# Attention and two expert layers on one core: sums of `s` in two runs, weight sums on VectorE, output products placed later, nine early products

## The chip, the core and the metric
The kernel runs on one core of a Trainium2 chip. The core has five engines that run side by side, each in the order of its own instructions: TensorE (products, "PE" in the profile), VectorE (DVE), ScalarE (ACT), GpSimd (POOL) and SyncE (SP, which here only issues transfers). Semaphores order them. The metric is device time in microseconds of one launch, measured outside the profiler; lower is better.

## The reference
```python
def _attn_ref(q, k, v, s):                     # (4, 8, 576, 64), s: (4, 8, 576)
    scores = scale * np.matmul(q, k.transpose(0, 1, 3, 2))
    cum = np.cumsum(np.maximum(s, 0.0), axis=-1)
    bias = -(cum[:, :, :, None] - cum[:, :, None, :])
    scores = np.where(causal, -1000000000.0, scores + np.minimum(bias, 0.0))
    ...
    attn = attn / (np.sum(attn, axis=-1, keepdims=True) + 1e-09)
    return np.matmul(attn, v)

x = attn_out as 2304 tokens of 512
h = np.maximum(x @ w_in, 0.0);  x = h * h @ w_out                        # w_in 512 x 2048
h = np.maximum(np.maximum(x @ w1, x @ w2), x @ w3);  out = h @ w_out2    # w1 512 x 768
```
The matrices of the two expert layers arrive as 64-bit words, which the kernel turns into pairs of tiles (a high and a low part).

## The kernel before, in words
**Attention.** The 32 heads are taken as 16 pairs. Each pair has nine units of query rows; `u_s` computes the scores of a unit on TensorE: first the product of `xq` and `xk`, and on top of it a product of `cq` and `ck` (line 646), three rows of bf16 parts of the cumulated sum of `s` for each head and three rows of constants, which adds the bias. `u_max` (VectorE), `u_exp` (ScalarE), `u_t` (transposes on TensorE), `u_et` (ScalarE) and `w_pv` follow; the numbers of `ORDER` set how many units each is late.

`setup` makes the sums. VectorE scales `s`, scans its 576 columns (32 heads on 32 partitions), and splits the result into three bf16 parts. The first pair gets its rows of `ck` and `cq` straight from these (`cum(parts)`: three transfers on SP's queue, three on ScalarE's). All parts are also stored to `c_dram`, and every later pair reads its rows from there. After that `v()` loads the pair's values, and `loads(1)` the second pair's keys, queries, rows of `c_dram` and values, all on SP's queue and in that order.

**Weights.** A weight tile is a job of nine to eleven stages: load of 64-bit words (`st`), four VectorE steps (`exponent` to `rest`, lines 397 to 408), a sum of two tiles (`whole`, line 415), ScalarE's cast to the high part (line 429), and a subtraction that leaves the low part (line 433). The sum and the subtraction run on `adder[0]`: GpSimd in the attention stage, VectorE after (`adder[0] = nc.vector` at the head of `experts`). `Slots` decides when the stages are issued. Jobs that are begun in the attention stage keep what `w_job` read when they were begun.

**First expert layer.** For each block of tokens and each block `f` of 128 hidden units, TensorE does twelve products into a bank (`h_products`, line 812), ScalarE and VectorE turn the bank into `hh` (lines 971 to 974: relu, square, high part, low part), and TensorE does twelve products of `hh` with `w_out` (line 995), two blocks later (`LAG`).

**Second expert layer.** Three groups of 768 tokens. A group has nine items (three weight matrices in three column pairs); an item has seven product steps of six products of 384 columns (line 1132), with 1, 5 and 2 copied out of their bank by ScalarE (`s1`, `s5`, `s2`) and added by VectorE. After its nine items a group has six output tiles of 128 tokens: `split_out` makes high and low part (`hh`), 18 products (line 1104) follow, the result is copied to `ob` and stored on SP's queue. `OUT2_AT` says between which steps of the next group's items an output tile stands: {item: {step: tile}}. The last group's tiles come at the end. `split_out` of a tile is issued after the tile ahead of it.

## Time and profile before
| | |
|---|---|
| runs | 847.57, 847.71, 850.11 us (median 847.71) |
| profiled execution | 847.02 us, of which the span of the core is 845.2 us |
| TensorE busy | 826.4 us (98%), 5284 products |
| VectorE, ScalarE, GpSimd busy | 524.3, 407.5, 175.4 us |
| attention, first layer, second layer, by TensorE's lines | about 0 to 174, 174 to 566, 566 to 842 us |

Times in the rows are microseconds from the start of the span unless marked ns. A row of a timeline has the start, the length, the engine, the line of the program, the operation, what it writes and reads by the program's names, the tile's size, and a count; in brackets stands how long the engine had been idle and what ended that. Rows of the same kind that follow each other are merged. SPq rows are issues of transfers; their length is the issue alone (or from the first issue to the end of the last, where several are merged). TensorE's products overlap, and their ends are modelled.

### The profile page before, as it was taken

Reading aid. Unit: us, or ns where it says so; the run is one execution under the profiler, and the core shown is the slowest. Engines: PE = TensorE matmul, PEld = TensorE weight load, DVE = VectorE, ACT = ScalarE, POOL = GpSimd, SP = SyncE. Lnnn points to the kernel's source line nnn. Section 1 sums busy time; section 2 is a strip of 40 time slices with the busy share of each in tenths; the row PEclk is TensorE's granted clock in tenths of the full one; section 3 lists DMA queues with packets and bytes.
Section 4 is the critical chain, followed back from the end, with each engine's and each line's share of the span. In section 5 each row is a group of like instructions: output and inputs, shape, how many; then the busy total and the mean of one; then the engine's idle time right before and its main releaser. Section 6 shows DMA issues by size and latency. Waiting matters only on the chain.

```text
span 845.2 us, 14494 instructions
## 1 busy us (share of the span) xinstructions
PE 826.4 (98%) x5284; PEld 700.5 (83%) x5284; DVE 524.3 (62%) x1103; ACT 407.5 (48%) x833; POOL 175.4 (21%) x273
## 2 busy tenths in 40 slices
PE   5999999999999999999999999999999999999998
PEld 3555565577888899999998888889998899899996
DVE  6777787749766656765877786843563335633442
ACT  5888889845544445445544555432242222421221
POOL 3054444544231323222123232100000000000000
PEclk9999999999999999999999999999999999999999
DMA  5565657453544454896758596639921573026602
GB/s 162 178 192 170 218 188 217 123 154 126 179 153 148 150 194 150 310 362 218 243 201 309 181 314 228 248 105 406 407 91 44 197 262 121 13 75 217 231 1 75
DMA packets 72631, 159.77 MB, mean 189 GB/s; under 512 B 12784, under 2 KB 32816, under 8 KB 72560
## 3 DMA queue, kind: packets, MB, share of 16 engines
q1 hardware_dynamic: 55764, 102.73, 36.1%
q0 software_dynamic: 16784, 56.11, 18.8%
q8 instruction: 41, 0.67, 0.3%
q14 instruction: 30, 0.25, 0.1%
q10 hardware_dynamic: 12, 0.01, 0.0%
HBM read 113.53 MB, written 45.27 MB: 188 GB/s over the span
## 4 chain that ended last, share of the span: by engine, by line
PE 91%; DVE 3%; ACT 2%; DMA 2%; POOL 1%; issue 0%; SPq 0%; DVEq 0%; ACTq 0%; POOLq 0%
PE banks L995 22%; PE banks L1132 13%; PE first L812 11%; PE banks L812 11%; PE banks L1104 9%; PE first L1132 8%; PE pairs L768 5%; PE pairs L723 3%; PE pairs L644 2%; PE pair L644 2%; PE pair L651 1%; ACT e L681 1%; DMA st<-in_w_in_dram 1%; PE pairs L651 1%; DVE hh L807 1%; PE pairs L646 1%
## 5 line engine op out<-in xcount | busy, mean ns | idle before, releaser
L995 PE MATMUL banks<-hh,sl 128*128 128x512 f32 (+1 forms) x960 | 210.1, 367 | 1.8 <-DVE hh L974 1.8
L995 PEld LDWEIGHTS banks<-hh,sl 128*128 128x128 f32 x960 | 175.1, 188 | 24.8 <-DVE hh L974 2.2
L1132 PE MATMUL banks<-xs,sl 128*128 128x384 f32 x702 | 131.2, 335 | 0.0
L1132 PEld LDWEIGHTS banks<-xs,sl 128*128 128x128 f32 x702 | 122.8, 188 | 0.9 <-DMA sl<-keep_p 0.2
L974 DVE TENSOR_TENSOR hh<-r,hh 128x512 fp32r<-128x512 f32 (+1 forms) x80 | 52.0, 651 | 98.8 <-ACT hh L973 98.6
L812 PE MATMUL first<-xs,sl 128*128 128x512 f32 (+1 forms) x432 | 93.6, 365 | 0.0
L812 PE MATMUL banks<-xs,sl 128*128 128x512 f32 (+1 forms) x432 | 93.6, 365 | 0.0
L681 ACT ACTIVATE e<-e,nm 128x128 f32<-128x128 f32 (+2 forms) x144 | 83.5, 585 | 10.0 <-DVE nm L667 9.9
L812 PEld LDWEIGHTS first<-xs,sl 128*128 128x128 f32 x432 | 78.6, 188 | 9.4
L812 PEld LDWEIGHTS banks<-xs,sl 128*128 128x128 f32 x432 | 78.6, 188 | 9.4
L1132 PE MATMUL first<-xs,sl 128*128 128x384 f32 x432 | 84.6, 335 | 0.3 <-DMA sl<-keep_p 0.3
L1104 PE MATMUL banks<-sl,hh 128*128 128x512 f32 (+1 forms) x342 | 78.4, 382 | 1.9 <-DVE hh L807 1.5
L1132 PEld LDWEIGHTS first<-xs,sl 128*128 128x128 f32 x432 | 75.8, 188 | 1.0 <-issue 0.6
L1104 PEld LDWEIGHTS banks<-sl,hh 128*128 128x128 f32 x342 | 61.4, 188 | 16.0 <-DVE hh L807 3.4
L971 ACT ACTIVATE r<-banks 128x512 f32<-128x512 f32 (+1 forms) x40 | 22.2, 556 | 91.6 <-PE banks L812 86.7
L971 ACT ACTIVATE r<-first 128x512 f32<-128x512 f32 (+1 forms) x40 | 22.2, 556 | 89.2 <-PE first L812 89.2
L1033 ACT COPY s<-first 128x384 f32<-128x384 f32 x36 | 17.2, 479 | 79.3 <-PE first L1132 79.2
L768 PEld LDWEIGHTS pairs<-et,xv 128*64 128x64 f32 (+1 forms) x448 | 27.8, 135 | 31.1 <-ACT e L681 8.9
L768 PE MATMUL pairs<-et,xv 128*64 128x320 f32 (+4 forms) x448 | 52.7, 367 | 0.0
L1033 ACT COPY s<-banks 128x384 f32<-128x384 f32 x45 | 21.6, 479 | 57.3 <-PE banks L1132 56.8
L972 ACT ACTIVATE r<-r 128x512 f32<-128x512 f32 (+1 forms) x80 | 47.2, 590 | 2.5
L973 ACT CAST hh<-r 128x512 fp32r<-128x512 f32 (+1 forms) x80 | 46.3, 579 | 2.5
(109 smaller groups left out, 1149.9 us busy)
## 6 DMA issues: line engine op xcount, KB each, us to landing
sl<-keep_p SPq DMA_DIRECT2D x68, 512.0 KB
st<-in_w_dram POOLq DMA_DIRECT2D x36, 256.0 KB, 5.7
st<-in_w_out_dram POOLq DMA_DIRECT2D x35, 256.0 KB, 3.9
sl<-keep_out SPq DMA_DIRECT2D x14, 512.0 KB
keep_p<-hi POOLq DMA_DIRECT2D x9, 768.0 KB, 5.2
keep_p<-sums POOLq DMA_DIRECT2D x9, 768.0 KB, 6.6
st<-in_w_in_dram POOLq DMA_DIRECT2D x22, 256.0 KB, 4.2
xk<-in_kT_dram SPq DMA_DIRECT2D x16, 288.0 KB
```

The lines of the kernel that those rows point to most:

```text
L644: nc.tensor.matmul(b[:, j, 0:w], lhsT=d["xq"][rows(j), w - P:w], rhs=d["xk"][rows(j), 0:w], start=True, stop=False)
L681: nc.scalar.activation(out=e_u[u][:, 0:w], in_=e_u[u][:, 0:w], func=ACTF.Exp, scale=-1.0, bias=st.pop(n), accum_out=sums[p, win][:, col:co ...
L768: nc.tensor.matmul(pv[rows(j), f:(W0, W1)[w]], lhsT=xv[0:kr, j, k, :], rhs=rhs, start=(k == 0), stop=(k == last))
L812: nc.tensor.matmul(hps[:, 0:n], lhsT=w[:, wp, kk * P:(kk + 1) * P], rhs=x[kk][xp][:, 0:n], start=(kk == 0 and c == 0), stop=(kk == KD - 1 ...
L971: nc.scalar.activation(out=r[:, 0:n], in_=hps[:, 0:n], func=ACTF.Relu)
L972: nc.scalar.activation(out=r[:, 0:n], in_=r[:, 0:n], func=ACTF.Square)
L973: nc.scalar.copy(out=hh[:, 0, 0:n], in_=r[:, 0:n])
L974: nc.vector.tensor_tensor(out=hh[:, 1, 0:n], in0=r[:, 0:n], in1=f32(hh[:, 0, 0:n]), op=ALU.subtract)
L995: nc.tensor.matmul(xacc[d][:, 0:n], lhsT=w[:, wp, d * P:(d + 1) * P], rhs=hh[:, xp, 0:n], start=(m == 0 and c == 0), stop=(end and c == 2))
L1033: nc.scalar.copy(out=x, in_=bank[:, 0:T2])
L1104: nc.tensor.matmul(b, lhsT=hh[g, t][:, hp_, q, h, :], rhs=w[:, wp, lo:hi], start=(begin and n == h == c == 0), stop=(end and n == len(f) - ...
L1132: nc.tensor.matmul(at[m, b][:, 0:T2], lhsT=w[:, wp, at_w + kk * P:at_w + (kk + 1) * P], rhs=x[:, kk, xp, :], start=(i in (0, 1, 3) and kk ...
```

## The change
Five edits.
- `setup`: the sums of `s` are made in two runs, columns 0 to 383 and 384 to 575 (`sums_to`, `FIRST_C`). The transfers of a part are issued as soon as it is there; the first pair's values are loaded between the runs.
- `setup`: nine products of a constant bf16 tile (512 columns) stand at the head of TensorE's program (`WARM`). Their result is not used; the bank is written anew by its first transposes.
- `w_job`: `adder[0]` is read when the sum runs.
- `OUT2_AT`, `split_out`: output tiles stand two to four steps later in the next group, and at the end the third tile is split ahead of the first one's last products.
- The pools: `s1`, `s5`, `s2` and `ob` share five buffers of 512 columns; `hh` of the second layer has three buffers.

```diff
@@ -21,6 +21,8 @@
 MAX_PAIRS = 0
 PUMP_FROM = 9
 PUMP_END = 0
+FIRST_C = 384
+WARM = 9
 PRE = 2
 PRE_X = (30, 21, 12, 5)
 PRE_AT = 1
@@ -44,7 +46,7 @@
 FAR = 24
 PACE_FAR = 3
 RR = 2
-OUT2_AT = {1: {0: 0, 4: 1}, 2: {1: 2, 5: 3}, 3: {0: 4, 2: 5}}
+OUT2_AT = {1: {2: 0, 6: 1}, 2: {3: 2}, 3: {0: 3, 4: 4}, 4: {1: 5}}
 LAG = 2
 MAX_OPEN = 3
 ST_BUFS = 3
@@ -421,8 +423,7 @@
         if i[0] == "P":
             return item_job(*i[1:])
         b = {}
-        add = adder[0]
-        first = words_of(i, b, lambda: (f32(b["a"]), add))
+        first = words_of(i, b, lambda: (f32(b["a"]), adder[0]))
 
         def high_part():
             b["h"] = t[:, 0, :] if t is not None else sums_tile()[:, 0:512].bitcast(F32R)
@@ -430,7 +431,7 @@
 
         def low_part():
             b["l"] = t[:, 1, :] if t is not None else b["a"].bitcast(F32R)
-            add.tensor_tensor(out=b["l"], in0=f32(b["a"]), in1=f32(b["h"]), op=ALU.subtract)
+            adder[0].tensor_tensor(out=b["l"], in0=f32(b["a"]), in1=f32(b["h"]), op=ALU.subtract)
 
         def store():
             for h, x in enumerate((b["h"], b["l"])):
@@ -556,6 +557,20 @@
         parts = st[2][0:BH, :].bitcast(BF16)[:, 0:3 * S].rearrange("p (r c) -> p r c", r=3)
         c8 = e_u[NU - 1][0:BH, 0:S]
         nc.sync.dma_start(out=sc, in_=s)
+
+        def sums_to(lo, hi, rest):
+            x, c, d = sc[:, lo:hi], c8[:, lo:hi], rest[0:BH, 0:hi - lo]
+            nc.vector.tensor_scalar(out=x, in0=x, scalar1=0.0, scalar2=8.0, op0=ALU.max, op1=ALU.mult)
+            nc.vector.tensor_tensor_scan(out=c, data0=one[:, lo:hi], data1=x, initial=c8[:, lo - 1:lo] if lo else 0.0,
+                                         op0=ALU.mult, op1=ALU.add)
+            nc.vector.tensor_copy(parts[:, 0, lo:hi], c)
+            cum(parts, 0, lo, hi)
+            nc.vector.tensor_tensor(out=parts[:, 1, lo:hi], in0=c, in1=parts[:, 0, lo:hi], op=ALU.subtract)
+            cum(parts, 1, lo, hi)
+            nc.vector.tensor_tensor(out=d, in0=c, in1=parts[:, 0, lo:hi], op=ALU.subtract)
+            nc.vector.tensor_tensor(out=parts[:, 2, lo:hi], in0=d, in1=parts[:, 1, lo:hi], op=ALU.subtract)
+            cum(parts, 2, lo, hi)
+
         k, q, cum, v = loads(0)
         k()
         q()
@@ -574,19 +589,18 @@
         nc.gpsimd.memset(cq[2], 0.0)
         for j in range(2):
             nc.gpsimd.memset(cq[2][D * j:D * j + 3, :], 1.0)
+        busy = e_u[5].bitcast(BF16)[:, 0:512]
+        nc.vector.memset(busy, 1.0)
+        for _ in range(WARM):
+            nc.tensor.matmul(pairs[0][:, 0, :], lhsT=busy[:, 0:P], rhs=busy, start=True, stop=True)
         nc.vector.memset(one, 1.0)
         nc.vector.memset(bound[:, 0:SQ - P], 0.0)
         nc.vector.memset(bound_l[:, 0:SQ], 0.0)
         nc.vector.memset(e_u[NU - 1][:, S:], 0.0)
-        nc.vector.tensor_scalar(out=sc, in0=sc, scalar1=0.0, scalar2=8.0, op0=ALU.max, op1=ALU.mult)
-        nc.vector.tensor_tensor_scan(out=c8, data0=one, data1=sc, initial=0.0, op0=ALU.mult, op1=ALU.add)
-        for r in range(3):
-            nc.vector.tensor_copy(parts[:, r, :], c8)
-            if r < 2:
-                nc.vector.tensor_tensor(out=c8, in0=c8, in1=parts[:, r, :], op=ALU.subtract)
-        cum(parts)
+        sums_to(0, FIRST_C, e_u[NU - 2])
+        v()
+        sums_to(FIRST_C, S, e_u[NU - 3])
         nc.sync.dma_start(out=c_dram, in_=parts)
-        v()
         for j in range(2):
             nc.vector.tensor_copy(bound_l[rows(j), SQ:S], bound[rows(j), SQ - P + D * j:SQ - P + D * (j + 1)])
 
@@ -604,14 +618,13 @@
             nc.sync.dma_start(out=d["xq"], in_=qT[p])
 
 
-        def cum(parts=None):
+        def cum(parts=None, i=0, lo=0, hi=S):
             for t, r, queue in ((ck[p % 3], 0, nc.sync), (cq[p % 3], 3, nc.sync if parts is None else nc.scalar)):
                 if parts is None:
                     for j in range(2):
                         queue.dma_start(out=t[D * j + r:D * j + r + 3, :], in_=c_dram[2 * p + j])
                 else:
-                    for i in range(3):
-                        queue.dma_start(out=t[r + i:r + i + D + 1:D, :], in_=parts[2 * p:2 * p + 2, i, :])
+                    queue.dma_start(out=t[r + i:r + i + D + 1:D, lo:hi], in_=parts[2 * p:2 * p + 2, i, lo:hi])
 
         def v():
             d["xv"] = hp.tile([P, 2, NKT, D], F32, tag="xv", name="xv")
@@ -1018,8 +1031,8 @@
         phS.close()
         slots.soon_kept = SOON_KEPT_2
         with ExitStack() as ph2:
-            r_p, hh_p, c_p, s_p, o_p = (ph2.enter_context(tc.tile_pool(name=n, bufs=b, reuse_waits="tile"))
-                                        for n, b in (("rr2", 2), ("hh2", 2), ("cc2", 1), ("ss2", 2), ("oo2", 2)))
+            r_p, hh_p, c_p, s_p = (ph2.enter_context(tc.tile_pool(name=n, bufs=b, reuse_waits="tile"))
+                                        for n, b in (("rr2", 2), ("hh2", 3), ("cc2", 1), ("ss2", 5)))
             rings = dict(X=Ring(banks[0:3]), Z=Ring(banks[3:5]), Y=Ring(banks[5:6]))
             ring_o = Ring(banks[6:8])
             where = {0: "X", 1: "Z", 2: "X", 3: "Y", 4: "X", 5: "Z", 6: "X"}
@@ -1029,7 +1042,7 @@
             tmp = {}
 
             def copied(m, name, bank):
-                x = tmp[m, name] = s_p.tile([P, T2], F32, tag=name, name=name)
+                x = tmp[m, name] = s_p.tile([P, DM], F32, tag="s", name="s")[:, 0:T2]
                 nc.scalar.copy(out=x, in_=bank[:, 0:T2])
 
             def after(m, i):
@@ -1105,7 +1118,7 @@
                                                  start=(begin and n == h == c == 0),
                                                  stop=(end and n == len(f) - 1 and h == 1 and c == 2))
                     if end:
-                        ob = o_p.tile([P, DM], F32, tag="ob", name="ob")[:, 0:hi - lo]
+                        ob = s_p.tile([P, DM], F32, tag="s", name="ob")[:, 0:hi - lo]
                         if (t + k) % 2:
                             nc.vector.tensor_copy(ob, b)
                         else:
@@ -1143,10 +1156,11 @@
                     if m == len(items) - 1 and i == 6:
                         for t in range(2):
                             split_out(last, t, order2[-1:])
+                        split_out(last, 2, range(NQ))
                 else:
                     _, g, t, f, begin, end = item
                     out_products(g, t, f, begin, end)
-                    ahead = t + (1 if g < last else 2)
+                    ahead = t + (1 if g < last else 3)
                     if end and ahead < 2 * T2 // P:
                         split_out(g, ahead, range(NQ))
                 slots.pos += 1
```

SP's queue at the start, before (the second pair's rows are `ck_170` and `cq_167`, read from `c_dram`):
```order
L600 DMA xk<-in_kT_dram 128x576
L604 DMA xq<-in_qT_dram 128x576
L614 DMA ck_169<-st 2x576 x3
L588 DMA c_dram<-st 32x1728
L618 DMA xv<-in_v_main_dram 128x2x256
L619 DMA xv<-in_v_tail_dram 64x2x64
L600 DMA xk<-in_kT_dram 128x576
L604 DMA xq<-in_qT_dram 128x576
L611 DMA ck_170<-c_dram 3x576 x2
L611 DMA cq_167<-c_dram 3x576 x2
```
And the same queue now:
```order
L618 DMA xq<-in_qT_dram 128x576
L627 DMA ck_169<-st 2x384 x3
L631 DMA xv<-in_v_main_dram 128x2x256
L632 DMA xv<-in_v_tail_dram 64x2x64
L627 DMA ck_169<-st 2x192 x3
L603 DMA c_dram<-st 32x1728
L614 DMA xk<-in_kT_dram 128x576
L618 DMA xq<-in_qT_dram 128x576
L625 DMA ck_170<-c_dram 3x576 x2
L625 DMA cq_167<-c_dram 3x576 x2
```
The store to `c_dram` has moved behind the value loads and behind three more transfers.

VectorE at the entry to the first expert layer, before (`wa` and `st` belong to weight jobs; `hh` is the low part that TensorE waits for):
```order
L397 TENSOR_SCALAR wa<-st 128x512
L401 SCALAR_TENSOR_TENSOR st<-st,wa 128x512
L405 TENSOR_SCALAR wa<-st 128x512
L408 SCALAR_TENSOR_TENSOR st<-st,wa 128x512
L397 TENSOR_SCALAR wa<-st 128x512
L401 SCALAR_TENSOR_TENSOR st<-st,wa 128x512
L974 TENSOR_TENSOR hh<-r,hh 128x512
L405 TENSOR_SCALAR wa<-st 128x512
L408 SCALAR_TENSOR_TENSOR st<-st,wa 128x512
L415 TENSOR_TENSOR wa<-st 128x512
L974 TENSOR_TENSOR hh<-r,hh 128x512
```
And now, at the same place:
```order
L407 TENSOR_SCALAR wa<-st 128x512
L410 SCALAR_TENSOR_TENSOR st<-st,wa 128x512
L417 TENSOR_TENSOR wa<-st 128x512
L399 TENSOR_SCALAR wa<-st 128x512
L403 SCALAR_TENSOR_TENSOR st<-st,wa 128x512
L987 TENSOR_TENSOR hh<-r,hh 128x512
L434 TENSOR_TENSOR sl_93<-wa,sl_93 128x512
L407 TENSOR_SCALAR wa<-st 128x512
L410 SCALAR_TENSOR_TENSOR st<-st,wa 128x512
L417 TENSOR_TENSOR wa<-st 128x512
L434 TENSOR_TENSOR sl_94<-wa,sl_94 128x512
L987 TENSOR_TENSOR hh<-r,hh 128x512
```
A sum (line 417) has come in ahead of the load that the next job waits for, and two subtractions (line 434) stand among the rows behind the first `hh`; all three ran on GpSimd before.

TensorE at the first output tile of a group, before (line 1104 is the output tile, line 1132 the next group's products):
```order
L1132 MATMUL banks_3002<-xs,sl_83 128x384 x6
L1132 MATMUL first_2885<-xs,sl_101 128x384 x6
L1104 MATMUL banks_3003<-sl_86,hh 128x512 x3
L1104 MATMUL banks_3003<-sl_96,hh 128x512 x3
L1104 MATMUL banks_3003<-sl_84,hh 128x512 x3
```
And now (line 1117 is the output tile):
```order
L1145 MATMUL banks_3023<-xs,sl_83 128x384 x6
L1145 MATMUL first_2906<-xs,sl_101 128x384 x6
L1145 MATMUL first_2905<-xs,sl_89 128x384 x6
L1145 MATMUL banks_3021<-xs,sl_87 128x384 x6
L1117 MATMUL banks_3024<-sl_86,hh 128x512 x3
L1117 MATMUL banks_3024<-sl_96,hh 128x512 x3
```
Two steps of six products now stand between the step that ends the group's results and the tile.

## Rows read from the trace of the kernel before

**Rows 1.** Busy time by stretch: us, busy (and count) of each engine, clock, DMA.
```profile
40.00:60.00 20.00, 20.00 (x246) 11.88 (x244) 15.83 (x60) 18.08 (x48) 11.89 (x14) 1.00 0.60 176
```

**Rows 2.** Timeline of TensorE, products that read `cq` of the first two pairs.
```profile
10.42 0.29 PE L646 MATMUL pairs<-ck,cq 64*128 64x128 bf16 x2 [4.69 <-DMA cq<-st]
...
17.05 0.22 PE L646 MATMUL pair<-ck,cq 64*128 64x128 bf16 x2
```

**Rows 3.** Timeline of TensorE, entry to the first expert layer.
```profile
190.76 2.88 PE L812 MATMUL first<-sl,sl 128*128 128x512 f32 x12
...
195.68 0.50 PE L995 MATMUL banks<-hh,sl 128*128 128x512 f32 x1 [1.82 <-DVE hh L974]
```

**Rows 4.** TensorE's waits over the span: us in total, times, longest.
```profile
PE banks L1104 <- DVE hh L807: 1.5, 3, 0.5
```

**Rows 5.** Timeline of VectorE, the sums of `s`.
```profile
2.70 0.70 DVE L581 TENSOR_SCALAR st<-st 32x576 f32<-32x576 f32 x1 [0.21 <-DMA st<-in_s_dram]
3.43 1.34 DVE L582 TENSOR_TENSOR_SCAN e<-st 32x576 f32<-32x576 f32 x1
4.81 0.52 DVE L584 CAST st<-e 32x576 bf16<-32x576 f32 x1
5.37 0.75 DVE L586 TENSOR_TENSOR e<-e,st 32x576 f32<-32x576 f32 x1
```

**Rows 6.** Timeline of SP's queue, first 14 us.
```profile
5.42 3.35 SPq L614 DMA_DIRECT2D ck<-st  x3
8.82 0.39 SPq L588 DMA_DIRECT2D c_dram<-st  x1
...
11.84 0.57 SPq L611 DMA_DIRECT2D ck<-c_dram  x2
12.51 0.55 SPq L611 DMA_DIRECT2D cq<-c_dram  x2
```

**Rows 7.** Busy time by stretch; the clock is third from the end.
```profile
12.00:13.00 1.00, 1.00 (x6) 0.26 (x5) 0.70 (x4) 0.61 (x3) 0.00 (x0) 1.00 0.89 239
```

**Rows 8.** TensorE by form, 0 to 14.5 and 14.5 to 30 us: busy us, mean ns.
```profile
L644 PE MATMUL pair<-xk,xq 64*128 64x256 f32 x4 | 1.2, 685 | 0.0
...
L644 PE MATMUL pairs<-xk,xq 64*128 64x256 f32 x4 | 0.7, 404 | 0.0
```

**Rows 9.** Timeline of VectorE, entry to the first expert layer.
```profile
188.83 0.69 DVE L401 SCALAR_TENSOR_TENSOR st<-st,wa 128x512 uint32<-128x512 uint32 x1
...
191.69 0.43 DVE L397 TENSOR_SCALAR wa<-st 128x512 uint32<-128x512 uint32 x1 [0.98 <-DMA st<-in_w_in_dram]
192.15 1.67 DVE L401 SCALAR_TENSOR_TENSOR st<-st,wa 128x512 uint32<-128x512 uint32 x1
193.74 1.89 DVE L974 TENSOR_TENSOR hh<-r,hh 128x512 fp32r<-128x512 f32 x1
```

**Rows 10.** Timeline of GpSimd at the same place.
```profile
191.78 1.48 POOL L433 TENSOR_TENSOR sl<-wa,sl 128x512 fp32r<-128x512 f32 x1
193.22 0.55 POOL L392 DMA_DIRECT2D st<-in_w_out_dram  x1
```

**Rows 11.** Timeline of TensorE, output tiles of the first group.
```profile
637.40 0.50 PE L1104 MATMUL banks<-sl,hh 128*128 128x512 f32 x1
638.39 4.17 PE L1104 MATMUL banks<-sl,hh 128*128 128x512 f32 x17 [0.49 <-DVE hh L807]
...
645.54 1.20 PE L1132 MATMUL first<-xs,sl 128*128 128x384 f32 x6
646.59 4.28 PE L1104 MATMUL banks<-sl,hh 128*128 128x512 f32 x18
...
675.65 4.68 PE L1104 MATMUL banks<-sl,hh 128*128 128x512 f32 x18
```

**Rows 12.** Timeline of TensorE, the end.
```profile
818.58 6.20 PE L1104 MATMUL banks<-sl,hh 128*128 128x512 f32 x25
825.27 16.62 PE L1104 MATMUL banks<-sl,hh 128*128 128x512 f32 x89 [0.49 <-DVE hh L807]
```

## The prediction, made before the changed kernel ran
> **What bounds the kernel now.** I read the table of busy time by stretch first, then the waits of TensorE, then the order of time on each engine at the places where TensorE waits. In the attention stage TensorE has no idle time at all: in the stretch 40 to 60 us it is busy for 20.00 of 20 us, while VectorE has 15.83 and ScalarE 18.08 [rows 1]. So what is won ahead of that stage is carried to its end, and what is won on VectorE or ScalarE inside it is worth nothing. The profiled execution took 847.02 us, 1.8 us more than its span of 845.2. Three places are left where TensorE stands still, and the change touches all three.
>
> The start: the first product that needs the sums of `s` runs at 10.42, after 4.69 us of waiting for the `cq` rows [rows 2]. The entry to the first expert layer: one product of L995 waits 1.82 us for VectorE's low part of `hh` [rows 3]. The output products of the second layer (L1104) wait three times, 1.5 us in all, for the low part of their split [rows 4].
>
> **The start.** Before, VectorE makes the sums of 576 columns in one run: 0.70 + 1.34 for the scaling and the scan, then casts of 0.52 and subtractions of 0.75 in turn [rows 5], and the third issue of `ck` parts ends at 5.42 + 3.35 = 8.77 [rows 6]. Now six instructions do 384 columns. If each shrinks with its columns, they take 0.47 + 0.90 + 0.35 + 3 x 0.50 = 3.2 us, and 3.4 with the gaps of 0.04 between rows; if none shrinks, 5.0. I take 3.6: a fixed part of 0.1 in each (the shortest row, 0.52, bounds it from above) keeps its last third, 0.2 in all. They begin at about 2.75, since 0.21 of the new memset of `busy` lies in the wait for `s` [rows 5], and the memset, half as many bytes as 512 of the columns that the subtraction takes 0.75 for, is hardly longer. That ends at 6.35, the third issue at about 6.85, 1.9 earlier, so the first product that needs the sums comes at about 8.5 instead of 10.42. Bounds: 0.5 and 2.1 us earlier.
>
> Behind it stands a second wait, which the change does not remove. The second pair needs its rows of `ck` and `cq` out of `c_dram`; the product that reads them ran at 17.05 [rows 2], and the SP queue had issued their transfers by 12.51 + 0.55 = 13.06 [rows 6]. From the end of the last issue to the product the first pair needed 10.42 - 8.77 = 1.65, so 14.7 is the earliest for these rows, and 2.35 us before 17.05 are slack. Now SP issues both value loads ahead of the second run's parts, then three more transfers, and only then `c_dram`. An issue takes 0.28 (two small ones in 0.57) to 0.66 (four loads between 8.82 + 0.39 and 11.84). By their sum (third part until 6.85, two loads 1.3, three parts 1.5) `c_dram` goes out at about 9.7 instead of 8.82, and the copies of it can't be read before it has landed: from its issue to the first reading issue were 11.84 - 8.82 = 3.0 before, and at least 0.39 + 1.65 = 2.0 are needed. So the reading issues begin between 11.7 and 12.7, against 11.84 before, and the second pair's product runs no sooner than 14.6 to 15.6. Its time of 17.05 can thus fall by 1.4 to 2.4, whatever the first pair gains. I take 1.9: the first pair's own gain, which also fits between those.
>
> The nine products. The rows say 1.00 for the granted clock in the stretch 12 to 13 [rows 7], which is the level of 2.4 GHz, yet the 256-column products after the wait take 685 ns and the same form later 404 [rows 8]; the engine had stood idle for 4.69 us before them. This form alone loses 0.5 us (1.2 against 0.7); if all of the 6.63 us from 10.42 to 17.05 were stretched so, it would be 2.7. Several forms around it are, not all: I estimate 1.9. The nine products themselves fall into a time in which TensorE waits, and would have to take 0.8 us each to reach 8.5. If they keep the later products at 404, the first pair ends up to 1.9 us sooner still, but then it meets the second pair's rows at 14.6 to 15.6, so I give them nothing. The bounds are 0 and, with rows at 14.6, 0.5; 1.9 only if the rows were free.
> The Trainium skill's "TensorE: Matmul & The Clock Gate", Part 1, says that the array is at the lower of its two levels by default and that sustained products release it; durations here agree with that (685 against 404 ns), the granted clock in the rows does not show it. By that rule alone the start would bring 3.8 us and the time would be 838.5.
>
> **The weight sums.** `adder[0]` is now read when the sum runs, so five sums of jobs begun in the attention stage go from GpSimd to VectorE, 0.69 each there (the size of the undisturbed L401 in the rows), 3.5 us on an engine that waits for loads in the same stretch. What they cost and give is read at one chain: VectorE waits until 191.69 for a piece of `w_in`, then L401 takes 1.67 and the low part of `hh` 1.89, where the same L401 took 0.69 three us earlier [rows 9]. Both lie beside work of GpSimd, a sum of 1.48 from 191.78 and what follows it [rows 10]. With these gone, L397, L401 and L974 end at 191.69 + 0.43 + 0.69 + 0.69 + 0.1 = 193.6. TensorE had issued the product ahead of the wait by 195.68 - 1.82 = 193.86 [rows 3], so the wait closes even if the load lands no sooner. One new sum stands in front of L397, but VectorE is idle for 0.98 there, which covers its 0.69. Behind the wait VectorE has two sums more before the next `hh`, 1.4 us; that `hh` is due only two groups of twelve products later, 5.5 us (190.76 to 193.5 for one) [rows 3]. Gain 1.8, between 0.6 (if the sums come out between the load and `hh`) and 1.9.
> A rule against this stands in "SBUF - State Buffer" of the Trainium skill, section "SBUF: two separate sides": a transfer issued by GpSimd has its descriptors written by that engine, which can be locked out of a port shared with VectorE for as long as some VectorE instructions run. The issue beside the 1.67 and 1.89 rows took 0.55 [rows 10], so the trace does not show it. By the rule each of three issues might wait 0.69; less a sum of 1.48 that no longer stands ahead of them, the load would land 0.6 later, the wait would be 0.3 instead of none, and the time 840.7.
>
> **The output products.** The first tile of a group now comes two product steps of six later, 2.1 us (645.54 to 646.59 for one); before, it took 0.50 + 0.49 + 4.17 = 5.16 us from 637.40 where an undisturbed one takes 4.28: 0.88 lost. The last tile of a group took 4.68, 0.40 lost; it now has four steps before it, not two [rows 11]. Two groups: 2.56. At the end 25 products stand between 818.58 and 825.27, 6.69 us against 25 x 4.28 / 18 = 5.94, so 0.75 is lost to the split of the third tile [rows 12]; its split is now queued before the first tile's last products instead of behind them, on a third buffer. Together 3.3; the rows that lead into the waits are stretched as well (0.2 to 0.3 at each of the three), so I take 3.6, between 1.5 (the idle time alone) and 4.3. The tail behind 825.27 is unchanged.
>
> **The sum.** 1.9 + 1.8 + 3.6 = 7.3 us. From the profiled 847.02 that is 839.7; the median of the runs shown, 847.71, lies 0.69 above that execution, and I carry this offset: 840.4.
>
> **Rivals.**
> The second pair's rows are not late, and the nine products pay: SP would have to read `c_dram` back about 2 us sooner than I count. For it: transfers of a few KB have the lines almost to themselves at that time. Against: three more issues and two loads are ahead. Then the start gives 3.8 and the time is 838.5.
> VectorE becomes the bound at the entry: the five sums come in front of an `hh` that TensorE needs, and a wait like the 1.82 stays. Against it is the working above. The time is 840.4 + 1.8 = 842.2. The same time comes out if the change does not do what it says at the start, because twelve short instructions take as long as seven long ones (5.0 against 3.6): 840.4 + 1.4 = 841.8.
> Slower: the copies `s1`, `s5`, `s2` and the output tiles `ob` now share five buffers, so that a ScalarE copy out of a bank can wait for the store of an output tile, and TensorE then waits for the bank. Twelve tiles in two groups have such followers. A follower comes about eight steps of 1.05 us behind, so a store has to take over 8.4 us to be felt; each us beyond that costs up to 12. The price passes the gain of 7.3 at stores of 9.0 us. At 9.3 it is 10.8 us and the time 851.2, slower by 3.5. Against it: nothing in the rows makes a store that long.
>
> **How the numbers follow.** Forecast 0.62; nine products pay 0.18; VectorE bound or the start in vain 0.13; shared buffers 0.04; the rest (0.03) is a mixture that ends near no change. What a measurement can tell from no change is 0.3%, 2.5 us, so 845.2 to 850.3 is "same". The first three cases are all below 845.2: faster 0.93, same 0.04, slower 0.03. For the range the ends are 847.71 less (2.3 + 1.9 + 4.3) = 839.2 and less (0.5 + 0.6 + 1.5) = 845.1; not all lower ends come together, and the rival at 838.5 is let in: 837.8 to 843.4.
>
> **What would show it.** Right: the first product on `cq` at 8.3 to 8.9; a wait of TensorE for `cq` or `xk` of the second pair until 14.6 to 15.6, if the early products are fast; no wait for the low part of `hh` near 190; no wait for the low parts at the three output places. Wrong: early 256-column products at 404 ns with no wait behind them (then the time is lower), any wait of ScalarE copies for a store, or a wait for `hh` at the entry.

## The result and the profile after

The changed kernel takes 840.28 us in the median (839.44 to 840.51), the kernel before 847.86 in the same comparison (847.57 to 850.11). The ratio is 0.9895, with a 95% interval of 0.9874 to 0.9917. The predicted time was 840.4. One execution of the run without products (2194.89 us) and one of the run with the outputs only (4669.16 us) took several times as long as all others and count in no ratio below (without them the medians of these two, 840.80 and 846.10, are 840.70 and 846.07).

The profiled execution has a span of 838.4 us, 6.8 less than before. TensorE's waits, as total, number and longest in us; [rows 4] has no counterpart any more, the output products (now L1117) don't wait:

```profile
PE pairs L659 <- DMA cq<-st: 2.9, 1, 2.9
...
PE first L1145 <- DMA sl<-keep_p: 0.7, 1, 0.7
...
PE banks L1008 <- DVE hh L987: 0.6, 1, 0.6
```

TensorE's timeline at the start (start, duration, line, operation, count, and the idle time before it) answers to [rows 2]:

```profile
1.47 3.85 PE L595 MATMUL pairs<-e 128*128 128x512 bf16 x9 [1.47 <-DVE e L593]
5.25 0.49 PE L657 MATMUL pairs<-xk,xq 64*128 64x128 f32 x4
8.62 0.29 PE L659 MATMUL pairs<-ck,cq 64*128 64x128 bf16 x2 [2.89 <-DMA cq<-st]
8.69 1.19 PE L657 MATMUL pair<-xk,xq 64*128 64x256 f32 x4
...
15.30 0.22 PE L659 MATMUL pair<-ck,cq 64*128 64x128 bf16 x2
```

The first pair's product comes 1.80 us earlier, the second pair's 1.75. The nine products (L595) end at 5.3, 2.89 us of idle time follow, and the 256-column products take 1.19 as they did without them [rows 8]. The granted clock, third from the end in the busy time by stretch, now shows this: half rate is 0.50, and the two middle stretches lie partly at it.

```profile
5.00:7.50 2.50, 0.74 (x6) 0.30 (x4) 2.40 (x6) 0.00 (x0) 2.07 (x4) 1.00 0.01 2
7.50:10.00 2.50, 1.38 (x10) 1.09 (x12) 1.85 (x10) 0.70 (x4) 0.00 (x0) 0.68 0.41 120
10.00:12.50 2.50, 2.50 (x16) 1.31 (x15) 1.55 (x7) 1.44 (x7) 0.00 (x0) 0.63 0.42 79
12.50:15.00 2.50, 2.50 (x36) 1.45 (x34) 1.72 (x7) 2.50 (x8) 0.00 (x0) 1.00 0.63 226
```

At the entry to the first expert layer, [rows 3] becomes a wait of 0.56. VectorE's timeline ahead of it, to be held against [rows 9], has no stretched operation, but a sum (L417) of 0.69 that GpSimd used to make, and no idle time between the load's arrival at 187.69 and `hh`. (The row at 187.69 names a transfer of `xr`, which L399 doesn't read; in the repeated profile below the same row names the weight load.)

```profile
192.48 2.83 PE L1008 MATMUL banks<-hh,sl 128*128 128x512 f32 x11 [0.56 <-DVE hh L987]
```
```profile
187.69 0.43 DVE L399 TENSOR_SCALAR wa<-st 128x512 uint32<-128x512 uint32 x1 [3.95 <-DMA xr<-x_at]
...
190.07 0.69 DVE L417 TENSOR_TENSOR wa<-st 128x512 f32<-128x512 f32 x1
190.68 0.42 DVE L399 TENSOR_SCALAR wa<-st 128x512 uint32<-128x512 uint32 x1
191.13 0.69 DVE L403 SCALAR_TENSOR_TENSOR st<-st,wa 128x512 uint32<-128x512 uint32 x1
191.74 0.69 DVE L987 TENSOR_TENSOR hh<-r,hh 128x512 fp32r<-128x512 f32 x1
```

The output tiles, against [rows 11, 12], all take 4.28 for 18, and the last 114 products run through:

```profile
636.49 4.28 PE L1117 MATMUL banks<-sl,hh 128*128 128x512 f32 x18
...
678.02 4.28 PE L1117 MATMUL banks<-sl,hh 128*128 128x512 f32 x18
...
812.80 22.19 PE L1117 MATMUL banks<-sl,hh 128*128 128x512 f32 x114
```

The kernels were run in four sets, each with its own runs of the kernel before: changed (before 847.86); no products, 21 products, 21 and values first, outputs only (before 849.01); weight sums only, two runs only, old places, changed again (before 848.42); 18 and values first, before with 27 products, sums undone (before 849.56). Whole times are compared inside a set.

From here on I read every profile by the same marks on TensorE's timeline, because the whole time of one kernel varies by more than some of the terms. "Pair 2" is the start of the second pair's first product on `cq`; "attention" runs from there to the first product of the first expert layer (L812 of before); "expert 1" from that to the start of the last product on `hh` of L995; "expert 2" from there to the end of the last output product. All in us:

| profile | first `cq` | pair 2 | attention | expert 1 | wait at entry | expert 2 |
|---|---|---|---|---|---|---|
| before | 10.42 | 17.05 | 147.5 | 400.9 | 1.82 | 276.4 |
| changed | 8.62 | 15.30 | 147.4 | 399.7 | 0.56 | 272.7 |
| changed, again | 8.66 | 16.45 | 147.4 | 400.7 | 1.58 | 272.2 |
| no products | 8.62 | 15.58 | 150.2 | 399.0 | none | 272.5 |
| 21 products | 8.65 | 14.99 | 147.3 | 398.8 | none | 272.4 |
| 21, values first | 8.80 | 14.61 | 147.9 | 398.8 | none | 272.1 |
| 18, values first | 8.32 | 14.41 | 149.0 | 398.8 | none | 272.4 |
| before with 27 products | 10.47 | 15.87 | 147.5 | 401.9 | 2.82 | 276.6 |
| two runs only | 8.60 | 16.65 | 152.0 | 401.3 | 2.27 | 276.6 |
| weight sums only | 10.42 | 17.77 | 147.3 | 399.8 | 0.70 | 276.6 |
| weight sums undone | 8.66 | 15.77 | 149.2 | 400.5 | 1.49 | 272.0 |
| outputs only | 10.43 | 18.07 | 148.7 | 403.1 | 2.39 | 272.4 |
| old places | 8.62 | 16.57 | 147.6 | 399.0 | none | 275.3 |

Between the first two rows that is 1.75 + 0.18 + 1.24 + 3.74, and the tail behind the last product is 0.10 longer: 6.8.

### The profile page after: what moved, and what is told of

Same layout as the page of the kernel before. It is cut to its first block, busy times and chain, and to the rows that moved or that the text cites. A ratio compares the mean times of both kernels' runs of the same rounds, so it can differ in the third digit from the quotient of the medians.

```text
span 838.4 us, 14535 instructions
## 1 busy us (share of the span) xinstructions
PE 827.7 (99%) x5293; PEld 701.7 (84%) x5293; DVE 525.0 (63%) x1114; ACT 407.7 (49%) x833; POOL 169.0 (20%) x268
## 4 chain that ended last, share of the span: by engine, by line
PE 94%; ACT 2%; DMA 2%; DVE 2%; issue 0%; SPq 0%
PE banks L1008 23%; PE banks L1145 14%; PE banks L825 11%; PE first L825 11%; PE banks L1117 9%; PE first L1145 9%; PE pairs L781 6%; PE pairs L736 3%; PE pairs L657 2%; PE pair L657 2%; PE pair L664 1%; DMA xr<-x_at 1%; PE pairs L664 1%; ACT e L694 1%; PE pairs L659 1%; DMA sl<-keep_p 1%
## 5 line engine op out<-in xcount | busy, mean ns | idle before, releaser
L1117 PE MATMUL banks<-sl,hh 128*128 128x512 f32 (+1 forms) x342 | 76.5, 379 | 0.0
L1117 PEld LDWEIGHTS banks<-sl,hh 128*128 128x128 f32 x342 | 61.7, 188 | 11.5
L1064 DVE TENSOR_TENSOR c<-banks,s 128x384 f32<-128x384 f32 x45 | 25.0, 556 | 42.9 <-PE banks L1145 42.7
```

Of the source, the lines that this page charges most:

```text
L1117: nc.tensor.matmul(b, lhsT=hh[g, t][:, hp_, q, h, :], rhs=w[:, wp, lo:hi], start=(begin and n == h == c == 0), stop=(end and n == len(f) - ...
```

## The experiments

**No products.** `WARM = 9` becomes `WARM = 0`.

> The changed kernel without the nine products of the constant tile (WARM = 0; the memset of the tile stays). Theory (they give nothing, because TensorE stands idle for 2.89 us behind them and the products from 8.62 on are slow again): time as the changed kernel, 840.3 within 0.5 us; the first product on cq stays near 8.6, the four 256-column products of the first pair take 1.19 us as there. Rival (they carry part of the gain at the start): 841.0 to 842.2, and the 256-column products or what follows them take longer than with the nine.

840.80 us, ratio 0.9901 (0.9878 to 0.9924). The first product on `cq` at 8.62, the 256-column products 1.19, pair 2 at 15.58; the theory holds: the nine are worth nothing that can be told (with them pair 2 lies at 15.30, 16.45, 16.57 and 15.77 in four profiles). The time lies at the upper end of my 840.3 within 0.5.

**21 products.** `WARM = 21`.

> The changed kernel with 21 products of the constant tile instead of nine, so that TensorE is busy from 1.47 to about 8.1 us and the idle time before the first product on cq is under 0.5 us. Theory (the second pair's rows are a wall close behind): the clock stays up, the four 256-column products take 0.7 to 0.8 us and not 1.19, TensorE reaches the second pair's cq product at about 14.0 instead of 15.30 and waits there until 14.6 to 15.3; the time falls by 0 to 0.7 us, 839.6 to 840.3. Rival without the wall: no wait, the second pair's product at 14.0, the time 839.0. Rival that the idle time is not what lowers the clock: the products from 8.6 on stay as slow as in the changed kernel, time 840.3.

838.95 us, ratio 0.9885 (0.9863 to 0.9906); its runs lie between 838.57 and 839.98.

```profile
1.47 6.12 PE L595 MATMUL pairs<-e 128*128 128x512 bf16 x21 [1.47 <-DVE e L593]
7.52 0.49 PE L657 MATMUL pairs<-xk,xq 64*128 64x128 f32 x4
8.65 0.23 PE L659 MATMUL pairs<-ck,cq 64*128 64x128 bf16 x2 [0.64 <-DMA cq<-st]
8.71 0.66 PE L657 MATMUL pair<-xk,xq 64*128 64x256 f32 x4
...
14.59 0.49 PE L657 MATMUL pair<-xk,xq 64*128 64x128 f32 x4 [0.60 <-DVE sm L704]
14.99 0.40 PE L659 MATMUL pair<-ck,cq 64*128 64x128 bf16 x2
```

With only 0.64 of idle time the 256-column products take 0.66. And the wall is there: TensorE stands still for 0.60 in front of the second pair. The row names VectorE's L704, whose result this product doesn't read; in the next run the same product begins at 14.10, ahead of L704 at 14.48, so it does not need it. It reads `xk` and `xq` of that pair, which SP issued between 10.88 and 11.79, so I take it for their transfer (the row doesn't show its landing). The next products, on `cq`, took 0.40 instead of 0.22. So the theory holds for the wall and its place (14.6 to 15.3); the wait came ahead of the pair's other product. The time does not fit it: 838.95 lies below the theory's 839.6 to 840.3, at the 839.0 of the rival without the wall. In its own set the run lies 1.8 below the one without products (840.70).

**21 products and the first pair's values first.** The two value loads `v()` are issued right behind `q()`, ahead of the sums, where SP has nothing to do.

> As the kernel with 21 products, and the first pair's two value loads are issued ahead of the sums (behind xk and xq, from 2.1 us) instead of between the two runs. Theory (the wall is set by the order of the SP queue): c_dram goes out 1.2 us earlier, near 9.2 instead of 10.39, the second pair's cq product runs at 13.9 to 14.2 without a wait, the time is 0.7 to 1.3 us below the changed kernel, 839.0 to 839.6. Rival: the value loads lie ahead of the sums' parts on the lines and the first product on cq comes later than 8.62, by up to 1 us; time 840.3 to 841.0. Rival (the wall was never there): same as the kernel with 21 products.

838.69 us, ratio 0.9883 (0.9861 to 0.9904).

```profile
8.80 0.22 PE L659 MATMUL pairs<-ck,cq 64*128 64x128 bf16 x2
...
14.10 0.49 PE L657 MATMUL pair<-xk,xq 64*128 64x128 f32 x4
14.61 0.40 PE L659 MATMUL pair<-ck,cq 64*128 64x128 bf16 x2
```
The load of `cq` into the array (PEld) names what it waited for:
```profile
14.60 0.27 PEld L659 LDWEIGHTS <-cq 64*128 64x128 bf16 x2 [0.20 <-DMA cq<-c_dram]
```

The wall moved 0.4 us and not the 1.2 by which `c_dram` goes out earlier (9.29 instead of 10.44): the reading issues begin at 11.82 instead of 12.38. The last reading issue ends at 13.03 instead of 13.59, and the product follows 1.57 behind it, 1.40 in the run before. The order of the queue is thus a part of the wall, less than I expected: I had put the product at 13.9 to 14.2, without a wait. The time lies below my 839.0 to 839.6. The 21 products here took 7.08 and reached past the first `cq` rows (8.80 instead of 8.65).

**The kernel before with 27 products**, nothing else changed:

```
+ busy = e_u[5].bitcast(BF16)[:, 0:512]
+ nc.vector.memset(busy, 1.0)
+ for _ in range(27):
+     nc.tensor.matmul(pairs[0][:, 0, :], lhsT=busy[:, 0:P], rhs=busy, ...)
```

> The kernel before with nothing changed but 27 products of a constant tile at the beginning, which keep TensorE busy from 1.47 to about 9 or 10 us, until shortly before its first product on cq at 10.42. Theory (the slow stretch behind the first wait costs 1.2 us where the clock rises early, 2.3 where it rises late): the four 256-column products take 0.66 and not 1.19, the second pair's cq product runs at 15.6 to 15.9 instead of 17.05 to 18.07, the time falls by 1.2 to 2.3 us. Rival (the second pair's rows are late here too): that product not before 16.5, gain under 0.6.

846.76 us, ratio 0.9972 (0.9956 to 0.9988).

```profile
10.52 0.66 PE L648 MATMUL pair<-xk,xq 64*128 64x256 f32 x4
...
15.87 0.22 PE L650 MATMUL pair<-ck,cq 64*128 64x128 bf16 x2
```

Pair 2 at 15.87, against 17.05, 17.77 and 18.07 in the three profiles without products and with the old sums: the slow stretch costs 1.2 to 2.2 us, as expected. My estimate in the prediction was 1.9. The median lies 2.8 below that of the kernel before in this set (849.56), more than the 1.2 to 2.3 expected; the interval (1.0 to 3.7) holds both.

**Two runs only.** The kernel before with `sums_to(0, 384)`, `v()`, `sums_to(384, S)`; `WARM = 0` (the memset of the tile stays).

> The kernel before with only the sums of s in two runs (384 and 192 columns), the value loads between the runs, and no products of a constant tile. Theory (the gain of the first pair is carried to the end, since TensorE never waits for the second pair's rows while its early products are slow): first product on cq at 8.6, second pair's at 15.3 to 15.6 instead of 17.05, the time 1.5 to 1.8 us below before. Rival (the SP queue's longer way to c_dram takes it back): second pair's product after 16.5, gain below 0.6.

847.63 us, ratio 0.9981 (0.9955 to 1.0006), which cannot be told from no change. The first product comes at 8.60, as expected; pair 2 at 16.65 is later than my 15.3 to 15.6 and lies where the rival put it, after 16.5. But it isn't the SP queue: the last reading issue ends at 13.52 here and at 13.54 in the changed kernel, and TensorE has no wait at the second pair. The four 512-column products of the first pair took 2.04 here and 1.17 in the changed kernel, that is, the rate rose later.

```profile
11.65 2.04 PE L658 MATMUL pair<-xk,xq 64*128 64x512 f32 x4
```

So how much of the 1.8 reaches the second pair depends on when the rate rises in that execution. The median gain, 0.8, is under my 1.5 to 1.8. The profile also lost 4.5 us in the attention stage, which the experiment doesn't touch: TensorE waited there for 4.8 us in all, 1.7 in the kernel before, and behind the longest of these waits it fell to half rate. The twenty products of L782 took 4.07; the same twenty take 2.42 in the run without products.

```profile
150.03 1.13 PE L658 MATMUL pair<-xk,xq 64*128 64x512 f32 x4 [1.73 <-DVE nm L681]
...
151.30 4.07 PE L782 MATMUL pairs<-et,xv 128*64 128x320 f32 x20
```
```profile
152.00:153.00 1.00, 1.00 (x8) 0.41 (x6) 1.00 (x4) 0.71 (x2) 0.45 (x1) 0.50 0.60 184
```

**Weight sums only.** `adder[0]` is read when the sum runs.

> The kernel before with only the part on the weight sums (the engine of a sum is read when the sum runs). Theory (the wait for hh at the entry closes or nearly closes): the wait falls from 1.82 in the recorded profile, 2.39 in the profile with the output products alone, to 0 to 0.6. Against a run of before whose clock stays up the gain is 1.3 to 1.9 us; where the wait of before lasts 2.4 us and TensorE is at half rate behind it (22 products lost 1.6 us there), the gain is up to 3.9. Median 1.3 to 3.0 below before, and a narrower spread of the runs than before's, with the granted clock of all of them at 0.999 or 1.0. Rival (the five sums that VectorE takes over stand in front of hh): the wait stays above 1.2 and the gain is below 0.6.

847.19 us, ratio 0.9989 (0.9966 to 1.0011). The wait is 0.70, just over the 0 to 0.6 expected and far from the rival's 1.2, and "expert 1" 399.8, 1.1 less than before. The median lies 1.2 below that of the kernel before (848.42), just under the 1.3 to 3.0 expected, and the interval holds no change too. The clock of three of the twelve runs is 0.998, which I had not expected either: they lie at 850.8 to 851.1, the other nine at 845.1 to 850.9. Alone, this run proves little.

**Weight sums undone** in the changed kernel (the engine is fixed when the job begins).

> The changed kernel with the part on the weight sums taken back (the engine of a sum is fixed when its job is begun, as before). Theory: from the first product of the first expert layer to its last product on hh it takes 400.9 to 403.1 us as in the three profiles without this part, not 398.8 to 400.7 as in the seven with it; the wait for hh at the entry is 1.8 to 2.4, and sums of GpSimd lie beside stretched VectorE operations (1.2 to 2.1 instead of 0.69). Time 1.2 to 3.6 us above the changed kernel: 841.5 to 844.5. Rival (the wait at the entry hangs on the load alone, and the part is worth nothing): 840 to 841.3, wait under 1.6.

842.57 us, ratio 0.9923 (0.9896 to 0.9950). The stretched operations are back, VectorE's beside GpSimd's:

```profile
189.83 0.43 DVE L399 TENSOR_SCALAR wa<-st 128x512 uint32<-128x512 uint32 x1 [3.18 <-DMA xr<-x_at]
...
192.55 1.41 DVE L403 SCALAR_TENSOR_TENSOR st<-st,wa 128x512 uint32<-128x512 uint32 x1
193.88 1.76 DVE L988 TENSOR_TENSOR hh<-r,hh 128x512 fp32r<-128x512 f32 x1
195.56 1.64 DVE L407 TENSOR_SCALAR wa<-st 128x512 uint32<-128x512 uint32 x1
```
```profile
192.26 1.16 POOL L417 TENSOR_TENSOR wa<-st 128x512 f32<-128x512 f32 x1 [4.48 <-DVE st L410]
193.37 1.72 POOL L435 TENSOR_TENSOR sl<-wa,sl 128x512 fp32r<-128x512 f32 x1
195.03 0.55 POOL L394 DMA_DIRECT2D st<-in_w_out_dram  x1
```

With 0.69 each, L403 and `hh` would end at 192.55 + 1.4 = 193.9 and not at 195.64, and the wait of 1.49 would not be: TensorE came to it at 194.21. The wait itself is below the 1.8 to 2.4 that I wrote and under the rival's 1.6, and "expert 1" at 400.5 lies just below my 400.9; the time fits my 841.5 to 844.5. The whole times of this set and the changed kernel's can't settle it, as their intervals overlap.

VectorE's chain can. From the L399 that waits for the load to the end of `hh` it takes 5.81 here (189.83 to 195.64) and 5.80 in the kernel before with 27 products; in all eight profiles with this part it takes 4.73 to 4.75 (187.69 to 192.43 in the changed kernel). So at the same arrival of the load the part is worth 1.07 us: 1.8 of stretching is gone, and the 0.69 of a sum has come in. In the other three profiles without it VectorE waits for a second load inside the chain (0.57, 0.98 and 1.42 us) and the chain takes 7.3 to 7.7; with it no profile does. "Expert 1" differs by more: the five profiles without this part have 400.5 to 403.1, mean 401.55; the eight with it 398.8 to 400.7, mean 399.31. That is 2.2 us on average, though 400.5 and 400.7 overlap. Beyond the 1.07 it hangs on when the loads land, and whether the part also makes them land sooner is not shown. At the entry all five without it have the stretched operations beside GpSimd's sums, the eight with it don't.

**Outputs only.** `OUT2_AT`, the pools and the earlier splits, on the kernel before.

> The kernel before with only the part on the output products of the second layer (their places, the third hh buffer, the shared pool of five, the earlier splits). Theory of the traces (3.0 us between the entry of the second layer and the last output products, 1.1 us in these): 4.1 us less than before, 843.6; none of the three waits for the low part. The recorded term was 3.6 (844.1), with 1.5 and 4.3 as its bounds. Rival (part of the difference seen there is owed to the other parts, by the later phase at which loads meet): less than 3.0, above 844.7.

846.10 us, ratio 0.9959 (0.9938 to 0.9979). "Expert 2" is 272.4 instead of 276.4, a gain of 4.0 as the theory has it, and no output product waits. The time fell by 2.9, which is under the rival's 3.0 (its interval is 1.8 to 5.3 and holds both). The profile speaks for the theory, since the stage itself shows the 4.0, and it shows where this one execution lost: pair 2 at 18.07, and a wait at the entry of 2.39 us behind which TensorE fell to half rate.

```profile
198.43 3.87 PE L995 MATMUL banks<-hh,sl 128*128 128x512 f32 x11 [2.39 <-DVE hh L974]
202.09 3.49 PE L812 MATMUL banks<-sl,sl 128*128 128x512 f32 x12
```
```profile
200.00:202.00 2.00, 2.00 (x6) 1.62 (x5) 2.00 (x5) 1.75 (x3) 1.07 (x2) 0.50 0.55 203
202.00:204.00 2.00, 2.00 (x7) 1.56 (x6) 1.94 (x4) 0.62 (x1) 0.00 (x0) 0.67 0.60 229
```

Eleven products took 3.87 where they take 2.79 after the wait of 2.27 in the profile of two runs only, twelve 3.49 instead of 2.88: 1.7 us on top of the wait.

**Old places.** The changed kernel with `OUT2_AT` of before; third buffer, shared pool and early splits stay.

> The changed kernel with the output products of the second layer at their old places in the group (OUT2_AT of before), everything else as changed (third hh buffer, shared pool of five, earlier splits of the last group). Theory: two waits of about 0.5 us for the low part come back, the two groups lose 2.6 to 3.0 us, the 114 products at the end still take 22.2; the time is 842.9 to 843.3 where the changed kernel has 840.3. Rival (the third buffer and the early splits carry it, not the places): 840.3 to 841.0, and no wait at the first tile of a group.

844.01 us, ratio 0.9949 (0.9928 to 0.9970).

```profile
635.16 0.50 PE L1117 MATMUL banks<-sl,hh 128*128 128x512 f32 x1
636.16 4.19 PE L1117 MATMUL banks<-sl,hh 128*128 128x512 f32 x17 [0.49 <-DVE hh L820]
...
673.44 4.62 PE L1117 MATMUL banks<-sl,hh 128*128 128x512 f32 x18
...
816.24 22.19 PE L1117 MATMUL banks<-sl,hh 128*128 128x512 f32 x114
```

Both group losses are back, the end stays repaired. The time is above my 842.9 to 843.3; the changed kernel of the same set has 841.25, and 2.8 above that is what I expected of the groups. By the marks, with 272.4 as the middle of the eight profiles that have the whole part, the places carry 275.3 - 272.4 = 2.9 and the earlier splits, with the third buffer and the shared pool, 276.6 - 275.3 = 1.3.

**Changed, again.**

> The changed kernel once more, in the same company as the others. Time 839.3 to 840.8 (0.989 to 0.991 of before); first product on cq at 8.6 and products at half rate behind it; the wait for hh at the entry between 0 and 0.6, the wait for the keep_p load near 570 between 0.2 and 0.7 (both hang on where a load lands in that execution). Rival (the 0.56 is inherent in the new order of VectorE, whose additional sum of 0.69 stands in front of hh): again 0.4 to 0.7.

841.25 us, ratio 0.9910 (0.9875 to 0.9944), runs from 839.13 to 844.28. The time lies just above my 839.3 to 840.8. Two things differ from the first profile.

```profile
1.47 4.02 PE L595 MATMUL pairs<-e 128*128 128x512 bf16 x9 [1.47 <-DVE e L593]
5.42 0.80 PE L657 MATMUL pairs<-xk,xq 64*128 64x128 f32 x4
...
11.71 2.04 PE L657 MATMUL pair<-xk,xq 64*128 64x512 f32 x4
...
194.71 2.81 PE L1008 MATMUL banks<-hh,sl 128*128 128x512 f32 x11 [1.58 <-DVE hh L987]
```
```profile
189.92 0.43 DVE L399 TENSOR_SCALAR wa<-st 128x512 uint32<-128x512 uint32 x1 [5.02 <-DMA st<-in_w_out_dram]
```

At the start the rate had not risen by the end of the nine products (0.80 for the four of 128 columns, not 0.49). At the entry the wait is 1.58, outside both of my expectations, with no stretched operation on VectorE: here it is a weight load that lands at 189.92.

**18 products, values first**, the candidate for the best version.

> The changed kernel with 18 products of the constant tile instead of nine, and the first pair's two value loads ahead of the sums on the SP queue. Meant as the best version. Theory (TensorE has no idle time over 1 us before the first product on cq in any execution, so the rate behind it is always the full one, and the second pair's rows land near 14.5): first product on cq at 8.6 to 8.7, second pair's at 14.4 to 14.6 (the changed kernel: 15.30 in one profile, 16.45 in another); time 838.2 to 838.9, 1.4 to 2.5 us below the changed kernel, runs within 2 us of each other. Rival (18 products are too few where the clock rises early; the idle time behind them lets it fall again): second pair's product at 15.3 to 16.6, time 839.5 to 841.

838.80 us, ratio 0.9877 (0.9853 to 0.9901), runs from 838.00 to 839.97. Pair 2 is at 14.41 and nothing waits for a late clock; expected were 14.4 to 14.6 and 838.2 to 838.9. The first `cq` product came at 8.32, ahead of my 8.6 to 8.7, with the values ahead of the parts. It, the version with 21 and values first (838.69) and the one with 21 (838.95) can't be told from each other. All their fifteen runs lie between 838.00 and 840.28, the changed kernel's ten between 839.13 and 844.28, but none of the three was run in a set with the changed kernel, and the intervals against before overlap. So the gain over the changed kernel rests on pair 2 (0.3 to 2.0 us earlier than in the changed kernel's two profiles) and on the 1.8 and 2.0 by which the two versions with 21 lie below the run without products in their set.

## Why the prediction was right

**The start** (1.9) was right in place and size: the first run of sums ended at 6.37 (6.35 worked out), the first product came at 8.62 (8.5), pair 2 gained 1.75. That the second pair shows so much of it is luck in part: in the other profile of the same program pair 2 is at 16.45, and in three profiles with the old sums and no products it is at 17.05 to 18.07. The wall (rows of the second pair at 14.6 to 15.6) was not met by the changed kernel, since its early products are slow; the run with 21 products met it at 14.6 to 15.0. So the argument was sound, but not what held the changed kernel back. One reason that I gave for the rival, that small transfers have the lines almost to themselves, was misread: [rows 7] has the DMA engines 89% busy from 12 to 13 us.

**The nine products** (nothing) have the right size, for a reason only half seen. I gave them nothing because of the wall. The runs show that they don't keep the rate at all: in the first profile it had risen at 5.25 and fell in the idle time of 2.89, in the repeated one it had not yet risen, and in the run with the sums undone it was still up for the first 256-column products (0.66) and fell behind them. The rival in which the clock pays, 838.5, is what 18 to 21 products reach: 838.7 to 839.0. I wrote that the granted clock in the rows does not show the lower level; before the change it doesn't, in the first profile with the nine products it does (0.68 and 0.63). In the repeated profile the rows read 1.00 from 10 to 14 us, where four 512-column products took 2.04 and not the 1.08 of the run with 21: at the start a 1.00 in the rows does not prove the full rate. The durations show the lower level: 3.85 / 9 = 428 ns for one of the nine, while 21 of them took 6.12 us and not 9.0. That the array starts at the lower of its two levels is what Part 1 of "TensorE: Matmul & The Clock Gate" in the Trainium skill has; the trace agrees.

**The weight sums** (1.8, no wait left) are the step that failed in part, and by my own sign, a wait for `hh` at the entry, it did. 1.26 of the 1.82 went in the first profile and 0.24 in the repeated one. I wrote that the new sum in front of L399 fits into 0.98 of idle time; but the first of the two loads came 4.2 us ahead of TensorE (187.69 against 191.93), not 5.5 (188.37 against 193.87) as before, VectorE had no such gap, and the 0.69 stood in front of `hh`. That is the rival "five sums in front of `hh`", at a third of its price. I also wrote that the wait closes even if the load lands no sooner; it does not, since with a chain of 4.74 the wait is whatever the load leaves of it (1.58 in the repeated profile, with the load 3.2 us ahead of TensorE). The stretched operations did vanish at the entry, and five of the eight profiles with this part have no wait. The 2.2 of all profiles is more than my 1.8, but only 1.07 of it is shown to be the part's own. The issues show no lock-out of GpSimd: one beside stretched operations took 0.55 in the run with the sums undone, and two took 1.06 at 191.06 in the changed kernel. The Trainium skill's rule on descriptor writing ("SBUF — State Buffer", section "SBUF: two separate sides") thus had no price that these rows show.

**The outputs** (3.6) brought 4.15: 3.03 from the groups (2.56 worked out) and 1.12 at the end (0.75 worked out). The term was undersized by a slip in its sum: to the 3.3 of whole rows I meant to add 0.2 to 0.3 at each of three places for the products that lead into a wait, which makes 3.9 to 4.2, and added 0.3 in all. The measured 4.15 fits the sum done rightly: 0.47 came on top in the groups and 0.37 at the end.

**Not foreseen**: the wait for the `keep_p` load near 570 grew from 0.29 to 0.70. In the repeated profile it is 0.2, in the other variants of the changed kernel at most 0.5, so I don't count it as an effect of the change. Shared buffers (851.2) cost nothing: no row names a copy that waited for a store, and TensorE waits for no bank.

The sum of 7.3 stands against 6.8 between the two profiles and 7.6 between the medians. In the profiles an output term that was 0.55 too small and an entry term 0.55 too large cancel; the `keep_p` wait is most of what is left. In the medians an offset comes in: the profiled execution of before lay 0.84 below its median, the changed one 0.10. So that the forecast hit 840.28 within 0.1 is luck; the repeated runs of the same program have 841.25. The range's ends were not all worked out either (the 2.3 for the start and the 843.4 follow from no bound given), but the result lies well inside any of them.

**Open**: in five of thirteen profiles the attention stage takes 148.7 to 152.0 instead of 147.3 to 147.9. In these five VectorE stands for 0.9 to 2.5 us behind a weight load at 145 to 149 us, in the other eight for at most 0.4, and the attention's row maxima (`nm`), for which TensorE waits, queue behind it. In the run without products:

```profile
147.63 0.43 DVE L399 TENSOR_SCALAR wa<-st 128x512 uint32<-128x512 uint32 x1 [2.33 <-DMA st<-in_w_out_dram]
```
```profile
148.80 1.13 PE L657 MATMUL pair<-xk,xq 64*128 64x512 f32 x4 [1.56 <-DVE nm L680]
```

My sentence that TensorE has no idle time in the attention stage thus holds for the stretch in [rows 1] and not for the stage: the kernel before waits 1.7 us there in all, and the kernel with two runs only 4.8. Why that load is late in some executions, and why the one at the entry is, was not settled. A fourth buffer for weight loads might tell; it wasn't tried.

## What to carry to other kernels

Products that are to keep TensorE's rate up should reach to the end of the wait, not only lie in front of it; here nine, with idle times of 2.4 to 3.1 us ahead of the first product on `cq`, were worth nothing, and 18 to 21, with 0.6 or less, moved the second pair forward by 0.3 to 2.0 us. Whether they also make the executions more alike is not shown. An engine that takes over work relieves the chain only if the work doesn't stand in front of the chain's own operations: count idle time by when the load arrives in the new order, not by the gap in the old one. Where executions differ by more than a term, read each profile by marks at the stages: the outputs' 4 us, half hidden in the whole time of one run, stand there with 0.7 of spread in the eight profiles that have them and 0.2 in the four that don't.

## What the runs showed of the hardware that was not expected

- How much a slow start costs differs from one execution to the next: the same four 512-column products of the first pair took 1.17 us in one profile of the changed kernel and 2.04 in the other, depending on when the rate rose. Part 1 of "TensorE: Matmul & The Clock Gate" in the Trainium skill says that the point differs from run to run; the trace agrees.
- The length of an idle time of TensorE alone did not tell whether half rate (0.50 in the rows) followed. It did behind 1.73 us (two runs only, at 150.03), 2.39 (outputs only, at 198.43), 2.44 (sums undone, at 8.66), 2.89 (changed, at 8.62) and 3.14 (old places, at 8.62); it did not behind 1.49 to 1.82, 2.27 and 2.82 us at the entry.
- At the entry an elementwise operation of VectorE beside a sum or subtraction on GpSimd took 0.8 to 2.0 us where it otherwise takes 0.4 to 0.7, and a subtraction on GpSimd (L433, L435) up to 1.7 where most take 1.3; a DMA issue by GpSimd beside it kept its 0.55. In the run with the sums undone L403 from 192.55 ends at 193.96, 0.54 behind the end of GpSimd's sum (192.26 + 1.16), and L407, which has one input, was stretched too (1.64). In "SBUF — State Buffer", section "SBUF: two separate sides", the Trainium skill has a port pair that VectorE and GpSimd hold in turn, each for a whole instruction, when VectorE's operation has two inputs in SBUF or runs in a mode that uses both ports; the rows agree for L403, and no row shows the mode of L407.
